# Hash-bucket attention with adapters: output turns by DMA, PSUM copies on VectorE, casts on GpSimd

## The chip, the cores and the metric

The kernel runs on one core of a Trainium2 chip. The metric is the device time of one execution in microseconds (us), lower is better. PE (TensorE), DVE (VectorE), ACT (ScalarE), POOL (GpSimd) and SP (SyncE) each work through their own instructions in order; an instruction that waits holds up all that stand behind it on its engine. SP, ACT and POOL also issue DMAs.

## The reference

There are 4 batches of 8 heads, 768 positions and 64 features a head. Each query and key gets a 6-bit bucket from the signs of its projections; a query attends only to keys of its own bucket. Then comes a mixture of 8 adapters of rank 16, of which each row uses its two best.

```python
q_bits = (np.einsum('bhsd,dk->bhsk', q, proj) > 0)
...
mask = q_bucket[:, :, :, None] == k_bucket[:, :, None, :]
scores = scale * np.matmul(q, k.transpose(0, 1, 3, 2))
scores = np.where(mask, scores, -1000000000.0)
...
attn = attn / (np.sum(attn, axis=-1, keepdims=True) + 1e-09)
x = np.matmul(attn, v)          # heads side by side: 3072 rows x 512
logits = x @ w_gate
topk = np.argpartition(-logits, K, axis=1)[:, :K]
...
delta[mask] += w[mask, k, None] * (z @ B[e])   # z = x[mask] @ A[e]
return (x + delta).astype(np.float32)
```

## The kernel before, in words

The 32 heads go through as 16 pairs (p = 0 to 15), four pairs to a batch. The program is written out by hand: `run` walks over pairs and, in each, over nine slots (s = 0 to 8), and the order in which the calls stand is the order on each engine.

In a slot, `score` (L281) makes 1024 columns of scores on PE, in a PSUM tile of which there are two, and ACT takes their exponential into P (L290). Nine slots make the 2 x 6 blocks of 128 keys by 768 queries of a pair. A score matmul has 71 rows: 64 of features, scaled, and 6 of signs with a constant beside them, so that one matmul gives both the product and the bucket match. These operands lie in `aug`, of which there are two.

Before a pair's scores can run, its q and k are loaded (`load`, two pairs or more ahead, on SP's queue; three buffers), turned on PE in three groups of four blocks (`trans` L208, into a PSUM tile of the pool `ps_t`, which has two), copied from PSUM into `qkT` (two groups by ACT at L222, one by DVE at L224), cast with a factor into `aug` (`cast` L245, two instructions on DVE), and hashed (`hash` L231): PE multiplies with the projections, DVE makes signs (L240) and SP issues four small DMAs that carry them into `aug` (L151).

The output of a head is P turned against v: `pvmm` (L299) works in one PSUM tile (pool `ps_v`, one buffer). v lies in `vb` (three buffers) with a column of ones for the row sums, and a seventh slot that holds the sum of v over the six blocks; `vcast` (L194) makes these on POOL. `pvmm` opens each head with a matmul of the constant `eps` with that seventh slot (L304), which gives the uniform term of rows that match nothing. `norm` (L306) takes the reciprocal of the sums and scales the output into `x` on DVE (L321, L323); after the second head POOL casts x to bf16 (`xb`, L330).

The adapters need x turned: `xtrans` (L353) turns six blocks on PE and copies them into `xT` on DVE (L365). One batch later, in pairs 4b+5 and 4b+6, `moe_slot` (L444) takes three row blocks a pair: `lgz` (logits and first factor, PE), `route_a` and `route_b` (top two and weights on DVE, a small exp on ACT), `zmtrans` (turn), `delta` (second factor, added to x by DVE, L435, and stored).

The last pair orders its queries otherwise, so that a third of the rows is done after three slots; `third` does its output, and the last batch's adapters follow in three groups of two blocks.

## Time and profile before

| | before |
|---|---|
| three runs, median (range) | 196.83 us (196.22 to 197.68) |
| profiled execution, its own time | 195.71 us |
| its span | 193.8 us |
| PE busy | 173.4 us (89%) |
| ACT busy | 159.2 us (82%) |
| DVE busy | 116.6 us (60%) |
| POOL busy | 66.1 us (34%) |
| DMA, mean | 136 GB/s |
| first score, first score of pairs 1, 2 and 15 | 13.0, 23.4, 33.2, 168.4 us |

Busy times come from one profiled execution; matmuls are pipelined and their ends are modelled, so PE's busy share overstates how much of it is used. Durations and starts are read from the groups of instructions, the timeline and the chain of waits. A group's line gives the source line, engine, operation, output and inputs, shapes and count, then the busy time in us and the mean in ns of one, and then the idle time of the engine just before them with what ended it. A line of the chain gives its start, its length and what ran.

### The profile page before, as it was taken

Reading aid. Unit: us, or ns where it says so; the run is one execution under the profiler, and the core shown is the slowest. Engines: PE = TensorE matmul, PEld = TensorE weight load, DVE = VectorE, ACT = ScalarE, POOL = GpSimd, SP = SyncE. Lnnn points to the kernel's source line nnn. Section 1 sums busy time; section 2 is a strip of 40 time slices with the busy share of each in tenths; the row PEclk is TensorE's granted clock in tenths of the full one; section 3 lists DMA queues with packets and bytes.
Section 4 is the critical chain, followed back from the end, with each engine's and each line's share of the span. In section 5 each row is a group of like instructions: output and inputs, shape, how many; then the busy total and the mean of one; then the engine's idle time right before and its main releaser. Section 6 shows DMA issues by size and latency. Waiting matters only on the chain.

```text
span 193.8 us, 5264 instructions
## 1 busy us (share of the span) xinstructions
PE 173.4 (89%) x2176; PEld 118.4 (61%) x2177; DVE 116.6 (60%) x267; ACT 159.2 (82%) x192; POOL 66.1 (34%) x104
## 2 busy tenths in 40 slices
PE   6898899999999999899999999999999999885741
PEld 5464667575766758465758667575758575664520
DVE  4537253637272787866363877783636968824682
ACT  3249899999999897989999998989999988877320
POOL 8189925151506060433333070606060340110000
PEclk9999999999999999999999999999999999999996
DMA  6809960707070706638251608366525221040224
GB/s 162 318 14 194 133 229 11 244 11 244 13 244 14 244 7 172 243 84 332 66 190 39 215 7 261 154 180 235 179 75 175 79 110 63 8 166 0 78 88 162
DMA packets 20953, 26.36 MB, mean 136 GB/s; under 512 B 6210, under 2 KB 19394, under 8 KB 20930
## 3 DMA queue, kind: packets, MB, share of 16 engines
q1 hardware_dynamic: 15950, 25.75, 40.0%
q0 software_dynamic: 4832, 0.27, 4.6%
q8 instruction: 17, 0.28, 0.6%
q14 instruction: 6, 0.05, 0.1%
q10 hardware_dynamic: 148, 0.01, 0.1%
HBM read 19.42 MB, written 6.29 MB: 133 GB/s over the span
## 4 chain that ended last, share of the span: by engine, by line
PE 39%; DVE 17%; ACT 13%; DMA 12%; issue 7%; POOL 6%; SPq 4%; POOLq 0%; DVEq 0%; ACTq 0%
PE s L288 15%; PE pv L295 10%; ACT P L290 9%; DMA nat<-in_k_dram 7%; PE tr L217 5%; DVE aug L249 4%; DMA vn<-in_v_dram 3%; ACT qkT L222 3%; PE xtp L363 3%; PE dl L433 2%; DVE x L323 2%; DVE qkT L224 2%; POOL wa L159 2%; PE pv L304 2%; DVE zm L404 2%
## 5 line engine op out<-in xcount | busy, mean ns | idle before, releaser
L290 ACT ACTIVATE P<-s 128x1024 bf16<-128x1024 f32 x144 | 141.4, 1037 | 14.1 <-PE s L288 13.4
L288 PE MATMUL s<-aug 71*128 71x256 bf16 (+1 forms) x396 | 85.9, 321 | 3.3 <-ACT P L290 2.2
L295 PEld LDWEIGHTS <-P 128*128 128x128 bf16 x1152 | 47.5, 98 | 11.0
L288 PEld LDWEIGHTS <-aug 71*128 71x128 bf16 x396 | 33.9, 98 | 25.2 <-issue 15.1
L295 PE MATMUL pv<-vb,P 128*128 128x65 bf16 x1080 | 47.5, 193 | 0.0
L330 POOL CAST xb<-x 128x768 bf16<-128x768 f32 x15 | 12.4, 825 | 99.4 <-DVE x L323 95.8
L249 DVE TENSOR_SCALAR aug<-qkT 64x1536 bf16<-64x1536 f32 x30 | 28.9, 965 | 10.0 <-ACT qkT L222 9.6
L217 PE MATMUL tr<-ident,nat 128*128 128x128 f32 x180 | 28.7, 278 | 1.2 <-DMA nat<-in_k_dram 1.2
L365 DVE COPY xT<-xtp 128x768 bf16<-128x768 bf16 (+1 forms) x17 | 8.9, 525 | 23.6 <-PE xtp L363 23.6
L217 PEld LDWEIGHTS tr<-ident,nat 128*128 128x128 f32 x180 | 19.9, 140 | 2.6 <-DMA nat<-in_k_dram 2.1
L435 DVE SCALAR_TENSOR_TENSOR acc<-dl,rt,x 128x512 f32<-128x512 f32 x24 | 17.8, 746 | 4.5 <-PE dl L433 3.8
L224 DVE COPY qkT<-tr 128x512 f32<-128x512 f32 x16 | 11.1, 691 | 12.1 <-PE tr L217 12.1
L323 DVE TENSOR_TENSOR x<-pv,ri 128x384 f32<-128x384 f32 x30 | 16.7, 557 | 1.2
L222 ACT COPY qkT<-tr 128x512 f32<-128x512 f32 x29 | 17.2, 595 | 0.0
L201 POOL TENSOR_TENSOR vs<-vn 128x384 f32<-128x384 f32 x16 | 16.0, 998 | 0.0
L199 POOL CAST vb<-vn 128x768 bf16<-128x768 f32 x16 | 13.3, 833 | 4.4 <-DMA vn<-in_v_dram 4.2
L240 DVE TENSOR_SCALAR sgn<-hs 128x384 bf16<-128x384 f32 x15 | 8.3, 552 | 7.7 <-PE hs L237 7.7
L237 PE MATMUL hs<-qkT,proj 128*32 128x384 f32 x120 | 12.8, 498 | 0.0
L304 PE MATMUL pv<-vb,eps 128*128 128x390 bf16 x30 | 10.0, 335 | 1.7 <-DVE x L323 1.7
L433 PE MATMUL dl<-Bcat,zmT 128*128 128x512 bf16 x23 | 8.6, 381 | 1.4 <-ACT zmT L423 0.5
L363 PE MATMUL xtp<-ident_bf,xb 128*128 128x128 bf16 x96 | 8.3, 219 | 1.5 <-DVE xb L351 0.8
L375 PE MATMUL lz<-wa,xT 128*128 128x136 bf16 x96 | 7.5, 223 | 0.3 <-DVE xT L365 0.2
(57 smaller groups left out, 111.3 us busy)
## 6 DMA issues: line engine op xcount, KB each, us to landing
vn<-in_v_dram SPq DMA_DIRECT2D x16, 384.0 KB
nat<-in_q_dram SPq DMA_DIRECT2D x15, 384.0 KB
nat<-in_k_dram SPq DMA_DIRECT2D x15, 384.0 KB
out_dram<-acc SPq DMA_DIRECT2D x6, 768.0 KB
out_dram<-acc SPq DMA_DIRECT2D x6, 256.0 KB
aug<-sgn SPq DMA_DIRECT2D x60, 9.0 KB
nat<-in_q_dram SPq DMA_DIRECT2D x2, 192.0 KB
nat<-in_k_dram SPq DMA_DIRECT2D x2, 192.0 KB
```

The costliest lines, as they stand in the source:

```text
L201: nc.gpsimd.tensor_add(out=s3, in0=vn[:, :, 0:3, :], in1=vn[:, :, 3:6, :])
L217: nc.tensor.transpose(out=ps[:, j * P:(j + 1) * P], in_=self.nat[p][:, idx % 2, idx // 2, u * P:(u + 1) * P], identity=self.ident)
L222: nc.scalar.copy(out=out, in_=ps)
L224: nc.vector.tensor_copy(out=out, in_=ps)
L249: self.nc.vector.tensor_scalar(out=self.aug[p % 2][0:64, :, e * n:(e + 1) * n], in0=self.qkT[p][64 * e:64 * e + 64, :].rearrange("p (j c) ...
L288: nc.tensor.matmul(out=ps[:, o:o + n], lhsT=aug[0:71, 2 * h + 1, kt * P:(kt + 1) * P], rhs=q, start=True, stop=True)
L290: nc.scalar.activation(out=self.P_[p][:, s * 1024:(s + 1) * 1024], in_=ps, func=ACT.Exp, scale=128.0)
L295: self.nc.tensor.matmul(out=pv, lhsT=self.p_at(p, h, kt, i), rhs=self.vb[p % 3][:, h, self.slot(kt), :], start=False, stop=(last and kt == ...
L304: self.nc.tensor.matmul(out=self.pv[p, h], lhsT=self.eps, start=True, stop=False, rhs=self.vb[p % 3][:, h, self.T, :].unsqueeze(1).to_broa ...
L323: nc.vector.tensor_tensor(out=self.x[b][:, :, c:c + D].rearrange("p (u e) d -> p e u d", e=2), in0=pv[:, :, 0:D].rearrange("p (e u) d -> p ...
L363: nc.tensor.transpose(out=ps[:, i * P:(i + 1) * P], in_=self.xb[b][:, sl, hp * P:(hp + 1) * P], identity=self.ident_bf)
L435: nc.vector.scalar_tensor_tensor(out=acc[:, i, :], in0=ps, scalar=self.rt[b, slots][:, i:i + 1], in1=self.x[b][:, slots[i], :], op0=ALU.mu ...
```

## The change

- All three groups of `trans` are copied by DVE, with the factor 2^-5 in the copy; `cast` becomes a plain copy with a change of type on POOL, both halves in slot 1.
- The uniform term leaves `pvmm`. `uniform` computes it once a pair in a small PSUM tile and copies it to SBUF on DVE; `norm` adds it to the PSUM output first.
- `xb` is laid out by pairs, and for pairs 0 to 13 `xturn`, a transposing DMA on SP's queue, takes the place of `xtrans`. It stands in slot 6, ahead of the pair's loads. Pairs 14 and 15 keep `xtrans`.
- `hash` moves from slot 4 to slot 2, the second norm from slot 3 to 4, the loads from slot 5 to 6.
- The adapters of the first two batches are spread over four pairs (2, 2, 1 and 1 blocks); the third batch keeps 3 and 3.
- At the start, the first head's signs go through POOL's and ACT's queues, and scores begin before the second head is hashed; the adapters' weights are loaded in slot 4 of pair 0 and not in slot 1.
- In the last pair `third` is cut in two parts, and the middle third has its PSUM tile in `ps_t`.

```diff
-        self.load_v(1)
 
...
-        turn(0)
+        self.turn0(0)
         for e in range(2):
-            nc.vector.tensor_copy(out=self.proj2[64 * e:64 * e + 64, e:12:2], in_=pst[64 * e:64 * e + 64, :])
-        half(0, 0, True)
+            nc.vector.tensor_copy(out=self.proj2[64 * e:64 * e + 64, e:12:2],
+                                  in_=self.pst[64 * e:64 * e + 64, :])
+        self.half0(0, 0, nc.scalar.copy)
         self.warm(5)
-        hashed(0)
-        half(0, 1, False)
-        turn(1)
-        self.warm(4)
-        hashed(1)
-        half(1, 0, True)
-        half(1, 1, False)
+        self.hash0(0, (nc.gpsimd, nc.scalar))
+        self.half0(0, 1, nc.vector.tensor_copy)
+        self.turn0(1)
+        self.half0(1, 0, nc.gpsimd.tensor_copy)
+        self.half0(1, 1, nc.gpsimd.tensor_copy)
...
-        self.warm(8)
+        self.warm(12)
+
+
+    def turn0(self, h):
+        nc, P = self.nc, self.P
+        for i in range(2):
+            ps = self.ps_s.tile([P, 384], F32, tag="s", name=f"trf{h}_{i}")
+            for u in range(3):
+                nc.tensor.transpose(out=ps[:, u * P:(u + 1) * P],
+                                    in_=self.nat[0][:, i, h, u * P:(u + 1) * P], identity=self.ident)
+            out = self.qkT[0][:, (2 * h + i) * 384:(2 * h + i + 1) * 384]
+            if i:
+                nc.scalar.mul(out, ps, 2.0 ** -5)
+            else:
+                nc.vector.tensor_scalar(out=out, in0=ps, scalar1=2.0 ** -5, scalar2=None, op0=ALU.mult)
+
+    def hash0(self, h, engs):
+        nc = self.nc
+        hs = self.ps_t.tile([self.P, 384], F32, tag="t", name=f"hsf{h}")
+        rows = slice(64 * h, 64 * h + 64)
+        for i in (2 * h, 2 * h + 1):
+            nc.tensor.matmul(out=hs[32 * i:32 * i + 32, :], lhsT=self.proj2,
+                             rhs=self.qkT[0][:, i * 384:(i + 1) * 384], start=True, stop=True)
+        sgn = self.sgp.tile([self.P, 384], BF16, tag="sgn", name=f"sgnf{h}")
+        nc.vector.tensor_scalar(out=sgn[rows], in0=hs[rows], scalar1=0.0, scalar2=0.5,
+                                op0=ALU.is_gt, op1=ALU.subtract)
+        for i in range(2):
+            self.sign_dma(engs[i], 0, 2 * h + i, sgn)
+
+    def half0(self, h, e, copy):
+        copy(out=self.aug[0][0:64, 2 * h:2 * h + 2, e * 384:(e + 1) * 384],
+             in_=self.qkT[0][64 * e:64 * e + 64, h * self.S:(h + 1) * self.S].rearrange("p (j c) -> p j c", j=2))
...
         out = self.qkT[p][:, g * 512:(g + 1) * 512]
         if on_act:
-            nc.scalar.copy(out=out, in_=ps)
+            nc.scalar.mul(out, ps, 2.0 ** -5)
         else:
-            nc.vector.tensor_copy(out=out, in_=ps)
+            nc.vector.tensor_scalar(out=out, in0=ps, scalar1=2.0 ** -5, scalar2=None, op0=ALU.mult)
...
-        self.nc.vector.tensor_scalar(
+        self.nc.gpsimd.tensor_copy(
             out=self.aug[p % 2][0:64, :, e * n:(e + 1) * n],
-            in0=self.qkT[p][64 * e:64 * e + 64, :].rearrange("p (j c) -> p j c", j=4),
-            scalar1=2.0 ** -5, scalar2=None, op0=ALU.mult)
+            in_=self.qkT[p][64 * e:64 * e + 64, :].rearrange("p (j c) -> p j c", j=4))
...
-    def pv_mm(self, pv, p, h, i, last):
+    def pv_mm(self, pv, p, h, i, start, last):
         for kt in range(self.T):
             self.nc.tensor.matmul(out=pv, lhsT=self.p_at(p, h, kt, i),
                                   rhs=self.vb[p % 3][:, h, self.slot(kt), :],
-                                  start=False, stop=(last and kt == self.T - 1))
+                                  start=(start and kt == 0), stop=(last and kt == self.T - 1))
 
     def pvmm(self, p, h, i0, i1):
         if p < 0:
             return
         if i0 == 0:
             self.pv[p, h] = self.ps_v.tile([self.P, self.T, self.D + 1], F32, tag="v", name=f"pv{p}_{h}")
-            self.nc.tensor.matmul(
-                out=self.pv[p, h], lhsT=self.eps, start=True, stop=False,
-                rhs=self.vb[p % 3][:, h, self.T, :].unsqueeze(1).to_broadcast([self.P, self.T, self.D + 1]))
         for i in range(i0, i1):
-            self.pv_mm(self.pv[p, h][:, i, :], p, h, i, i == self.T - 1)
+            self.pv_mm(self.pv[p, h][:, i, :], p, h, i, True, True)
+
+
+    def uniform(self, p):
+        n = self.D + 1
+        ps = self.ps_t.tile([self.P, 2, n], F32, tag="t", name=f"un{p}")
+        self.nc.tensor.matmul(out=ps, lhsT=self.eps, rhs=self.vb[p % 3][:, :, self.T, :], start=True, stop=True)
+        self.uni[p] = self.smallp.tile([self.P, 2, n], F32, tag="uni", name=f"uni{p}")
+        self.nc.vector.tensor_copy(out=self.uni[p], in_=ps)
 
     def norm(self, p, h):
         if p < 0:
...
-            self.xb[b] = self.xp.tile([P, T, self.Dm], BF16, tag="xb", name=f"xb{b}")
+            self.xb[b] = self.xp.tile([P, self.PPB, T, P], BF16, tag="xb", name=f"xb{b}")
             self.xT[b] = self.xp.tile([P, self.nD, self.S], BF16, tag="xT", name=f"xT{b}")
         pv = self.pv[p, h]
+        nc.vector.tensor_tensor(out=pv[:, 0:T, :], in0=pv[:, 0:T, :],
+                                in1=self.uni[p][:, h:h + 1, :].to_broadcast([P, T, D + 1]), op=ALU.add)
         ri = self.smallp.tile([P, T], F32, tag="ri", name=f"ri{p}_{h}")
-        nc.vector.reciprocal(out=ri, in_=pv[:, :, D])
+        nc.vector.reciprocal(out=ri, in_=pv[:, 0:T, D])
         c = (2 * hp + h) * D
         nc.vector.tensor_tensor(
             out=self.x[b][:, :, c:c + D].rearrange("p (u e) d -> p e u d", e=2),
-            in0=pv[:, :, 0:D].rearrange("p (e u) d -> p e u d", e=2),
+            in0=pv[:, 0:T, 0:D].rearrange("p (e u) d -> p e u d", e=2),
             in1=ri.rearrange("p (e u) -> p e u", e=2).unsqueeze(3).to_broadcast([P, 2, T // 2, D]),
             op=ALU.mult)
         if h == 1:
-            c = 2 * hp * D
-            nc.gpsimd.tensor_copy(out=self.xb[b][:, :, c:c + 2 * D], in_=self.x[b][:, :, c:c + 2 * D])
-
-
...
-    def third(self, u):
+            nc.gpsimd.tensor_copy(out=self.xb[b][:, hp], in_=self.x[b][:, :, hp * P:(hp + 1) * P])
+
+
+
+    def third(self, u, part):
         nc, P, T, D = self.nc, self.P, self.T, self.D
         p, b = self.n_pairs - 1, self.B - 1
-        pv = self.ps_v.tile([P, 2, 2, D + 1], F32, tag="v", name=f"pvl{u}")
-        nc.tensor.matmul(
-            out=pv, lhsT=self.eps, start=True, stop=False,
-            rhs=self.vb[p % 3][:, :, T, :].unsqueeze(2).to_broadcast([P, 2, 2, D + 1]))
+        if part == 0:
+            pool, tag = (self.ps_t, "t") if u == 1 else (self.ps_v, "v")
+            pv = pool.tile([P, 2, 2, D + 1], F32, tag=tag, name=f"pvl{u}")
+            ri = self.smallp.tile([P, 2, 2], F32, tag="ri", name=f"ril{u}")
+            self.pvl[u] = pv, ri
+            nc.tensor.matmul(
+                out=pv, lhsT=self.eps, start=True, stop=False,
+                rhs=self.vb[p % 3][:, :, T, :].unsqueeze(2).to_broadcast([P, 2, 2, D + 1]))
+        pv, ri = self.pvl[u]
         for h in range(2):
+            kts = range(T) if h == 0 else range(2) if part == 0 else range(2, T)
+            if h == 0 and part:
+                continue
             for e in range(2):
-                self.pv_mm(pv[:, h, e, :], p, h, 3 * e + u, h == 1 and e == 1)
-        ri = self.smallp.tile([P, 2, 2], F32, tag="ri", name=f"ril{u}")
-        nc.vector.reciprocal(out=ri, in_=pv[:, :, :, D])
-        self.pvl[u] = pv, ri
-        self.third_x(u, self.xb[b])
+                for kt in kts:
+                    nc.tensor.matmul(out=pv[:, h, e, :], lhsT=self.p_at(p, h, kt, 3 * e + u),
+                                     rhs=self.vb[p % 3][:, h, self.slot(kt), :], start=False,
+                                     stop=(part == 1 and e == 1 and kt == T - 1))
+        if part:
+            nc.vector.reciprocal(out=ri, in_=pv[:, :, :, D])
+            self.third_x(u, self.xb[b][:, self.PPB - 1])
 
     def third_x(self, u, dst):
-        D, c = self.D, 2 * (self.PPB - 1) * self.D
+        D = self.D
         pv, ri = self.pvl[u]
         self.nc.vector.tensor_tensor(
-            out=dst[:, 2 * u:2 * u + 2, c:c + 2 * D].rearrange("p e (h d) -> p h e d", h=2),
+            out=dst[:, 2 * u:2 * u + 2, :].rearrange("p e (h d) -> p h e d", h=2),
             in0=pv[:, :, :, 0:D], in1=ri.unsqueeze(3).to_broadcast([self.P, 2, 2, D]), op=ALU.mult)
+
+    def xturn(self, p):
+        if p < 0:
+            return
+        b, hp = p // self.PPB, p % self.PPB
+        self.nc.sync.dma_start_transpose(
+            out=self.xT[b][:, hp, :].rearrange("p (t c) -> p t c", t=self.T),
+            in_=self.xb[b][:, hp].rearrange("p t c -> p (t c)"))
 
     def xtrans(self, p, slots=tuple(range(6)), on_act=False):
         if p < 0:
...
             nc.tensor.transpose(out=ps[:, i * P:(i + 1) * P],
-                                in_=self.xb[b][:, sl, hp * P:(hp + 1) * P], identity=self.ident_bf)
+                                in_=self.xb[b][:, hp, sl, :], identity=self.ident_bf)
         (nc.scalar.copy if on_act else nc.vector.tensor_copy)(
...
-        if s == 0:
+        if b < 0 or b > self.B - 2:
+            return
+        groups = ((0, 1), (2, 3), (4,), (5,)) if b < self.B - 2 else ((0, 1, 2), (3, 4, 5))
+        if g >= len(groups):
+            return
+        slots = groups[g]
+        if s == 1:
             self.lgz(b, slots)
-        if s == 1:
             self.route_a(b, slots)
+        if s == 2:
             self.route_b(b, slots)
         if s == 3:
             self.zmtrans(b, slots)
-        if s in (5, 6, 7):
+        if 0 <= s - 5 < len(slots):
             self.delta(b, slots, s - 5)
 
...
+                if p == 0:
+                    self.first_pair(s)
+                else:
+                    self.pair(p, s)
                 self.moe_slot(p, s)
-        p, b = N - 1, self.B - 1
+        self.last_pair(N - 1, self.B - 1)
+
+    def first_pair(self, s):
+        if s == 0:
+            self.hash0(1, (self.nc.sync, self.nc.sync))
+            self.load_v(1)
+        if s < 3:
+            self.trans(1, s)
+        if s == 3:
+            self.cast(1, 0)
+            self.cast(1, 1)
+            self.load(2)
+        if s == 4:
+            self.hash(1)
+            self.uniform(0)
+            self.load_moe()
+        if s == 5:
+            self.vcast(1)
+            self.load(3)
+        if s == 6:
+            self.pvmm(0, 0, 0, 2)
+            self.trans(2, 0)
+        if s == 7:
+            self.pvmm(0, 0, 2, 4)
+            self.trans(2, 1)
+        if s == 8:
+            self.pvmm(0, 0, 4, 6)
+
+    def pair(self, p, s):
+        if s == 0:
+            self.norm(p - 1, 0)
+            self.trans(p + 1, 2)
+        if s == 1:
+            self.pvmm(p - 1, 1, 0, 2)
+            self.cast(p + 1, 0)
+            self.cast(p + 1, 1)
+        if s == 2:
+            self.hash(p + 1)
+        if s == 3:
+            self.uniform(p)
+            self.pvmm(p - 1, 1, 2, 5)
+        if s == 4:
+            self.pvmm(p - 1, 1, 5, 6)
+            self.norm(p - 1, 1)
+            self.trans(p + 2, 0)
+        if s == 5:
+            self.vcast(p + 1)
+            self.trans(p + 2, 1)
+        if s == 6:
+            self.pvmm(p, 0, 0, 2)
+            self.xturn(p - 1)
+            self.load(p + 3)
+        if s == 7:
+            self.pvmm(p, 0, 2, 4)
+        if s == 8:
+            self.pvmm(p, 0, 4, 6)
+
...
                 self.norm(p - 1, 1)
             if s == 3:
                 self.xtrans(p - 1)
+                self.third(0, 0)
             if s == 4:
-                self.third(0)
+                self.third(0, 1)
             if s == 5:
                 self.xtrans(p, t[0])
-                self.third_x(0, self.x[b])
+                self.third_x(0, x)
                 self.lgz(b, t[0])
             if s == 6:
                 self.route_a(b, t[0])
+                self.third(1, 0)
                 self.route_b(b, t[0])
             if s == 7:
+                self.third(1, 1)
                 self.zmtrans(b, t[0], last=True)
-                self.third(1)
-                self.delta(b, t[0], 0, last=True)
             if s == 8:
                 self.xtrans(p, t[1])
-                self.delta(b, t[0], 1, last=True)
+                self.delta(b, t[0], 0, last=True)
                 self.lgz(b, t[1])
-                self.third_x(1, self.x[b])
+                self.third_x(1, x)
         self.route_a(b, t[1])
+        self.third(2, 0)
+        self.delta(b, t[0], 1, last=True)
         self.route_b(b, t[1])
-        self.third(2)
         self.zmtrans(b, t[1], last=True)
+        self.third(2, 1)
+        self.delta(b, t[1], 0, last=True)
         self.xtrans(p, t[2], on_act=True)
-        self.delta(b, t[1], 0, last=True)
         self.lgz(b, t[2])
+        self.delta(b, t[1], 1, last=True)
         self.route_a(b, t[2])
-        self.third_x(2, self.x[b])
+        self.third_x(2, x)
         self.route_b(b, t[2])
-        self.delta(b, t[1], 1, last=True)
         self.zmtrans(b, t[2], last=True)
         for i in range(2):
             self.delta(b, t[2], i, last=True)
```

## The prediction, made before the changed kernel ran

> **What bounds the kernel now.** I read the stretches of two plain pairs and one adapter pair first (columns: stretch, length, then busy us and count of PE, PEld, DVE, ACT, POOL, and clock, DMA share, GB/s).
>
> ```profile
> 33.30:43.10 9.80, 9.40 (x126) 6.41 (x124) 5.03 (x9) 9.46 (x12) 3.47 (x5) 1.00 0.38 126
> 43.10:52.90 9.80, 9.56 (x126) 6.42 (x124) 5.03 (x9) 9.47 (x12) 3.47 (x5) 1.00 0.40 127
> 63.20:74.00 10.80, 10.67 (x143) 7.33 (x141) 8.63 (x23) 9.81 (x12) 3.47 (x5) 1.00 0.35 114
> ```
>
> A pair without adapter work takes 9.80 us with ScalarE busy 9.46 of them: ScalarE sets it. With adapter work it takes 10.8, PE busy 10.67: PE sets it. VectorE and GpSimd have room (5.0 and 3.5 of 9.8). Then the groups of instructions:
>
> ```profile
> L290 ACT ACTIVATE P<-s 128x1024 bf16<-128x1024 f32 x144 | 141.4, 1037 | 14.1 <-PE s L288 13.4
> L249 DVE TENSOR_SCALAR aug<-qkT 64x1536 bf16<-64x1536 f32 x30 | 28.9, 965 | 10.0 <-ACT qkT L222 9.6
> L222 ACT COPY qkT<-tr 128x512 f32<-128x512 f32 x29 | 17.2, 595 | 0.0
> L323 DVE TENSOR_TENSOR x<-pv,ri 128x384 f32<-128x384 f32 x30 | 16.7, 557 | 1.2
> L330 POOL CAST xb<-x 128x768 bf16<-128x768 f32 x15 | 12.4, 825 | 99.4 <-DVE x L323 95.8
> ```
>
> In a row without gaps exps start every 0.96 us (three in 2.88 in the timeline), so ScalarE's floor in a pair is 9 x 0.963 + 2 copies x 0.48 = 9.63. Last, the chain of waits in pair 7 (start, length):
>
> ```profile
> 92.67 0.45 PE s L288 x2
> 93.12 0.66 SPq L151
> 93.78 0.05 issue
> 93.83 0.72 SPq L151
> 94.56 0.05 issue
> 94.61 0.43 SPq L182
> 95.04 0.05 issue
> 95.09 4.28 DMA nat<-in_k_dram
> 99.37 0.04 issue
> 99.42 0.33 PE tr L217
> ```
>
> SP, which computes nothing, is on the chain: four sign DMAs at 0.72 us each stand ahead of the loads, and the load of k lands just as PE wants to turn it, 4.3 to 5.0 us after its issue. This queue has little slack already.
>
> **What the Trainium skill says.** "VectorE: DVE Perf Modes", The three transpose paths, prices a 128x128 bf16 turn at 1309 ns on the crossbar. "DMA: Bandwidth & Descriptors", Latency and other measured facts, gives a DMA transpose 261 GB/s where the middle dimension isn't contiguous. No DMA transpose is in the trace of before, so nothing here confirms either. "GPSIMD Engine Reference", Engine selection, says that one-input work on GpSimd runs at about line rate and that GpSimd can't reach PSUM. The trace agrees on the rate: the 128x768 cast took 825 ns, 1.07 ns an element.
>
> **The change part by part.** A pair's time zero is PE's start of its first score. PE distances are start to start.
>
> *ScalarE.* All 29 qkT copies leave it, two a pair (0.48 each beside exps): floor 9.63 -> 8.67.
>
> *PE.* From the chain and timeline a plain pair is 9 x 0.435 scores (3.9), 72 x 0.0305 pv (2.2), 3 x 0.475 turns (1.43), hash 0.88, two eps matmuls x 0.17 (0.34), six output turns 0.33: 9.0. Gone are 84 of 96 output turns and 30 eps matmuls of 390 columns. A 130-column one per pair is new (not in the trace; 0.06 to 0.17, I take 0.1). 9.0 - 0.33 - 0.34 + 0.1 = 8.5. Three adapter slots cost 1.45 (12 lz 0.65, ztp 0.17, dl 3 x 0.21), so two cost 1.0 and one 0.5.
>
> *VectorE.* Gone: 28.9 of casts and 14 xT copies x 0.56 = 7.8. New: 29 qkT copies x 0.69 = 20, 30 adds over 390 PSUM elements at 0.56 to 0.62 (row L323 has 384 elements in 0.557) = 18, 15 small uniform copies about 4, four more adapter groups about 4. 116.6 - 36.7 + 46 = 126, some 7.5 us of a 9.6 us pair: not a bound, but each norm grows from 0.8 to about 1.45 us and PE's next pv group waits for it. Two scores and one turn group, 1.4 us, cover that. In PE-bound pairs about 0.3 stays.
>
> *GpSimd.* Two casts of 64x1536 a pair. Between the 293 ns for 128 elements (ident_bf) and 825 for 768 a further element costs 0.83 ns, so 1.5 us each, at worst 2.0. A pair holds 3.0 + 0.83 + 2.75 (v) = 6.6 us. Queued behind the casts is xb, then v's sums.
>
> *Two-engine pace.* Before, the floor of 9.63 became 9.80, and PE's 10.45 in adapter pairs became 11.1 (six from about 10.6 to 11.5). Now ScalarE 8.67 and PE 8.5 lie level, so I take 9.1 for a plain pair, 9.9 with two slots, 9.4 with one, 10.6 with three (bubbles of 0.4 to 0.5; in them the adapters' small exp, which now follows its logits in the same slot, so that the big exps queue behind it). Pairs 2 to 14 hold 3, 4, 4 and 2 of these: 27.3 + 39.6 + 37.6 + 21.2 = 125.7, against 135.2 now (33.18 to 168.42).
>
> *The turned output in SP's queue.* The signs are issued two slots earlier. Hash at 2.4 to 2.9 plus 0.8, sgn 0.56, four issues 3.13: SP is free at about 7.3. The second norm starts after slot 4 (4.5), x ends at 6.2, and the 0.83 cast puts xb at 7.1. So the turn is issued at 7.3, and behind it in SP's order stand this pair's loads. With I for its issue and D for what it delays the loads in the DMA engines: 7.3 + I + 0.48 (q issue) + 4.7 (k landing, mean of 4.28, 4.84, 4.96) + D = 12.5 + x, x = I + D. PE wants that k 4.4 us into the next pair, so a pair lasts **at least 8.1 + x**. Bounds of x: a plain issue is 0.43 and 197 KB at 261 GB/s are 0.75, of which 0.43 hides behind q's own issue: 0.75. At the other end six turns of 1309 ns one after the other: 7.9. Between: 768 pieces of 256 B at the price of the trace's small packets (row q0, 4832 packets at 4.6% of 16 engines' span, 30 ns each) are 1.4 us, so I 0.45 + D 1.0, and I take **x = 1.5**, a floor of 9.6: 3 x 9.6 + 4 x 9.9 + 4 x 9.6 + 2 x 10.6 = 128.0. **Saved in pairs 2 to 14: 7.2.** The adapters read the turned rows four slots after the turn, about 4 us, in pairs 5, 9 and 13 the tightest, so a landing below 4 us costs nothing there.
>
> *The start.* Two separate PSUM tiles end PE's 0.65 wait for the copy between the first turns, and the first score no longer waits for the second head's hash: it goes at about 10.8, not 13.0 (its q signs now by GpSimd's queue, where a small issue took 0.92 and landed in 2.4; v 1's load, moved behind, is wanted only at 24). It is given back: the adapters' weight loads (0.92 + 4.12 + 0.89 of GpSimd) now come after two casts and ahead of v's cast for pair 1. GpSimd: second head's halves to 11.7, v 0 to 15, casts to 18.1, weight loads to 24.0, v 1 to 26.8. PE's uniform matmul of pair 1 stands in slot 3 and waits for that, some 3.5 us. The next score then goes at 27.0, where before it went at 27.65. Five slots at 0.98 against 5.53 us: pair 2 starts at 31.9 against 33.18. **Saved: 1.2.**
>
> *Last pair and tail* (25.4 us). Two longer norms ahead of PE's turn of pair 14: +1.3. The thirds start a slot earlier and in another buffer: the exps of this pair, 8.7 us of work, took 13.8, and of these gaps I give back 2.0. **Saved: 0.7** (between 3 and -1.5).
>
> Sum: 1.2 + 7.2 + 0.7 = 9.1. The profiled execution took 195.71 us (span 193.8 and 1.9 around it): 186.6. The three runs shown lie 0.5 to 2.0 above it, median 1.1, so **187.5**.
>
> **Rivals.**
> *A (forecast), chance 0.33*: x between 1.1 and 2, 185 to 193.
> *B, loads never late, 0.24*: x below 1.1. The pairs keep 125.7, saved 11.4, and with smaller bubbles (13 x 0.25) some 14: 181 to 185. For it: the byte rate. Against: a norm, a cast and an issue now stand ahead of each load.
> *C, a wash, 0.11*: x near 2 with casts of 2 us, which put xb 1 us later (floor 9.1 + x = 11.1): 194 to 199.
> *D, slower, 0.32*: the turn holds SP or the DMA engines, and k of the pair after next lands late in every pair, seen by PE at the first turn group. Break-even: (135.2 + 1.9) / 13 = 10.55, so it decides **from x = 2.4**. At x = 4 pairs 2 to 14 take 157, which makes 216. At 7.9 they take 208, 267. For it: the page's 1309 ns, the chain above, and small pieces: in 64 B ones, as the adapters' weights come, 3072 at 30 ns over 16 engines are 5.8 us. Against: the byte rate above.
>
> Within 1% is what a measurement of this kernel can't tell from no change. Faster gets A, B and a part of C, 0.60; same 0.08; slower 0.32. The range goes from 179 (B with a better tail) to 215, leaving out about 0.03 below and 0.16 above. Case A alone spans 185 to 193.
>
> **What would show it.** ScalarE's busy time near 143 us with no qkT copy, VectorE near 126, GpSimd near 113, some 100 fewer PE instructions in the pairs. Right: PE's wait for nat in slot 4 below 1 us a pair, and one PE wait of about 3.5 us for vb near 23 us. Wrong: the turn's issue row over 2 us, waits of PE's turn group for nat over 2 us a pair, a wait of lz for xT in pairs 5, 9 and 13, or casts far from 1.5 us.

## Result and profile after

The changed kernel takes 204.2 us (median; 203.22 to 205.68), the kernel before 196.79 us (196.22 to 197.68) on the same chip. The ratio is 1.038, with a 95% interval of 1.029 to 1.046: **slower**. The forecast was 187.5 us and faster. A ratio here and below is taken from those runs of a kernel that lie within 1.5% of its fastest, a median from all its runs.

The profiled execution of the changed kernel took 203.36 us, its span is 201.6 (before: 193.8). With PE's first score of pairs 2 and 15 as the cuts, the 7.8 us come from all three stretches:

| us | before | after | difference | forecast |
|---|---|---|---|---|
| up to pair 2 | 33.18 | 34.54 | +1.4 | -1.2 |
| pairs 2 to 14 | 135.2 | 139.5 | +4.2 | -7.2 |
| last pair and tail | 25.3 | 27.5 | +2.2 | -0.7 |

The stretches of a plain pair, a pair with two adapter blocks and one with one (columns: stretch, length, busy us and count of PE, PEld, DVE, ACT, POOL, then clock, DMA share, GB/s):

```profile
34.54:43.51 8.97, 8.81 (x118) 6.18 (x119) 5.30 (x12) 8.68 (x10) 6.39 (x8) 1.00 0.56 161
61.43:73.25 11.82, 9.96 (x129) 6.91 (x130) 8.72 (x23) 9.10 (x11) 7.36 (x10) 1.00 0.58 140
85.10:95.55 10.45, 9.35 (x122) 6.52 (x124) 7.96 (x21) 8.96 (x11) 5.55 (x6) 1.00 0.51 165
```

Plain pairs fell from 9.80 to 8.97 us, below the forecast. With two adapter blocks a pair takes 11.8 and PE is busy for only 10.0 of it: PE is idle for 1.9 us, ACT for 2.7. Before, the first adapter pair, with three blocks, took 11.04 us from first score to first score (62.62 to 73.66), and PE was busy for 10.91. So within pairs 2 to 14 the loss sits in pairs that have adapter work, of which there are now eight in the first two batches instead of four, and it is waiting, not work. The groups that answer those shown of before, with the new add (L324) and the adapters' weights, which the program calls `gw` (L427 now, L403 before; the line of before comes first):

```profile
L403 DVE TENSOR_TENSOR gw<-m,e 128x24 f32<-128x24 f32 x6 | 1.1, 182 | 1.2 <-ACT e L393 1.2
L289 ACT ACTIVATE P<-s 128x1024 bf16<-128x1024 f32 x144 | 141.9, 1023 | 32.3 <-PE s L287 29.6
L249 POOL CAST aug<-qkT 64x1536 bf16<-64x1536 f32 x30 | 43.8, 1460 | 21.8 <-DVE qkT L224 20.9
L224 DVE TENSOR_SCALAR qkT<-tr 128x512 f32<-128x512 f32 x45 | 29.6, 682 | 5.7 <-PE tr L217 5.5
L324 DVE TENSOR_TENSOR pv<-pv,uni 128x390 f32<-128x390 f32 x30 | 17.2, 573 | 21.3 <-PE pv L294 21.2
L427 DVE TENSOR_TENSOR gw<-m,e 128x16 f32<-128x16 f32 (+2 forms) x13 | 8.2, 633 | 1.1 <-ACT e L417 1.1
```

The casts take what they were forecast to (1460 ns). L427 doesn't: it multiplies 8 to 24 numbers a partition and took 182 ns for 24 before; now its mean is 633 and its longest 1070. ScalarE's wait for scores grew from 13.4 to 29.6 us. PE's longest waits (who waits, for whom, us in all, times, the longest), first one line of before:

```profile
PE ztp L419 <- DVE zm L404: 3.4, 4, 1.4
PE ztp L443 <- DVE zm L428: 10.6, 12, 2.2
PE dl L457 <- DVE acc L459: 4.9, 5, 1.0
PE tr L217 <- DMA nat<-in_k_dram: 2.1, 1, 2.1
PE xtp L387 <- POOL xb L335: 1.2, 1, 1.2
```

The wait for `zm` grew from 3.4 to 10.6 us; 3.0 and 4.2 of these lie in the last pair and tail, so in pairs 2 to 14 it grew from 0.4 to 6.4. The chain of waits through the adapter pair that starts at 61.43 (start, length, what; it reads from the hash to the turn of zm, then from a turn of a later pair's blocks to the adapters' second product):

```profile
64.21 0.83 PE hs L237 x8
65.03 0.02 issue
65.06 0.04 DVE sgn L240
65.09 0.44 issue
65.53 0.85 DVE gw L427
66.39 0.02 issue
66.41 0.43 DVE zm L428
66.84 0.05 issue
66.89 0.28 PE ztp L443 x2
...
68.70 0.45 PE tr L217 x4
69.15 1.27 DVE qkT L224 x2
70.42 0.67 DVE acc L459
71.09 0.04 issue
71.13 0.38 PE dl L457
```

Two pieces of VectorE are on the chain. `gw` (L427) lasts 0.85 us. And `acc` (L459), which must read the first product out of the one adapter buffer in PSUM before PE may make the second, stands behind two `qkT` copies of 1.27 us together, which the change put on VectorE.

The queue of SP in a plain pair, where the prediction feared the turn (start, length, line, operation):

```profile
47.30 3.18 SPq L151 DMA_DIRECT2D aug<-sgn  x4
50.83 2.01 SPq L375 DMA_TRANSPOSE xT<-xb  x1
52.88 0.58 SPq L182 DMA_DIRECT2D nat<-in_q_dram  x1
53.51 0.46 SPq L182 DMA_DIRECT2D nat<-in_k_dram  x1
```

The 14 issues of the turn have a median of 1256 ns, this one is the longest. After pair 0 PE never waited for `nat`: even here, q and k issued at 52.88 and 53.51 are turned from 57.22 to 57.85 (the load of k thus lands within some 4.3 us).

Why `gw` is long shows when VectorE's and GpSimd's timelines are laid side by side. First VectorE (start, length, line, operation), in three pairs:

```profile
64.18 0.16 DVE L414 TENSOR_TENSOR m<-lz,top 128x16 f32<-128x16 f32 x1
65.53 0.84 DVE L427 TENSOR_TENSOR gw<-m,e 128x16 f32<-128x16 f32 x1
88.98 1.07 DVE L427 TENSOR_TENSOR gw<-m,e 128x8 f32<-128x8 f32 x1
110.80 0.17 DVE L427 TENSOR_TENSOR gw<-m,e 128x16 f32<-128x16 f32 x1
```

And GpSimd at the same times:

```profile
63.37 2.98 POOL L249 CAST aug<-qkT 64x1536 bf16<-64x1536 f32 x2 [0.80 <-DVE qkT L224]
87.05 2.98 POOL L249 CAST aug<-qkT 64x1536 bf16<-64x1536 f32 x2 [2.23 <-DVE qkT L224]
107.83 2.98 POOL L249 CAST aug<-qkT 64x1536 bf16<-64x1536 f32 x2 [0.98 <-DVE qkT L224]
```

The casts end at 66.35, 90.03 and 110.81. The first two `gw` end at 66.37 and 90.05, the third starts as the casts end and takes its normal 0.17; with half the elements the second takes longer than the first, since it had longer to wait. Of the ten `gw` of pairs 5 to 14 eight are long (0.61 to 1.07 us); all eight start during the second cast of a pair and end 20 to 36 ns after it. The profiler's spans on GpSimd are rough, so no more should be read from these nanoseconds. `m` (L414), in the midst of the first casts, takes its normal 0.16; it has one input in PSUM, while both inputs of `gw` are in SBUF. The Trainium skill, "GPSIMD Engine Reference", Specifications, says that GpSimd's SBUF interfaces are shared with VectorE, with contention for VectorE instructions that have two SBUF inputs. This trace agrees with that, and adds the size: `gw` is held until the cast that runs beside it has ended.

### The profile page after: what moved, and what is told of

The parts are those of the page before. It is cut to its first block, busy times and chain, and to the rows that moved or that the text cites. A ratio compares the mean times of both kernels' runs of the same rounds, so it can differ in the third digit from the quotient of the medians.

```text
span 201.6 us, 5215 instructions
## 1 busy us (share of the span) xinstructions
PE 168.3 (84%) x2072; PEld 116.0 (58%) x2078; DVE 128.4 (64%) x324; ACT 148.0 (73%) x166; POOL 111.0 (55%) x137
## 4 chain that ended last, share of the span: by engine, by line
PE 52%; DVE 19%; POOL 9%; issue 8%; DMA 7%; ACT 2%; SPq 1%; POOLq 0%; DVEq 0%
PE s L287 21%; PE pv L294 9%; PE tr L217 7%; PE hs L237 5%; DVE gw L427 4%; DMA nat<-in_k_dram 3%; DMA xT<-xb 3%; DVE acc L459 3%; DVE zm L428 3%; PE lz L399 3%; POOL vs L201 3%; DVE qkT L224 2%; POOL vb L199 2%; PE ztp L443 2%; POOL xb L335 2%
## 5 line engine op out<-in xcount | busy, mean ns | idle before, releaser
L289 ACT ACTIVATE P<-s 128x1024 bf16<-128x1024 f32 x144 | 141.9, 1023 | 32.3 <-PE s L287 29.6
L287 PE MATMUL s<-aug 71*128 71x256 bf16 (+1 forms) x396 | 88.0, 326 | 3.9 <-issue 1.0
L249 POOL CAST aug<-qkT 64x1536 bf16<-64x1536 f32 x30 | 43.8, 1460 | 21.8 <-DVE qkT L224 20.9
L294 PEld LDWEIGHTS <-P 128*128 128x128 bf16 x1080 | 43.5, 98 | 16.5 <-DVE x L329 6.4
L224 DVE TENSOR_SCALAR qkT<-tr 128x512 f32<-128x512 f32 x45 | 29.6, 682 | 5.7 <-PE tr L217 5.5
L324 DVE TENSOR_TENSOR pv<-pv,uni 128x390 f32<-128x390 f32 x30 | 17.2, 573 | 21.3 <-PE pv L294 21.2
L217 PEld LDWEIGHTS tr<-ident,nat 128*128 128x128 f32 x180 | 21.2, 142 | 5.6 <-DMA nat<-in_k_dram 2.3
L459 DVE SCALAR_TENSOR_TENSOR acc<-dl,rt,x 128x512 f32<-128x512 f32 x24 | 17.8, 747 | 5.6 <-PE dl L457 4.5
L201 POOL TENSOR_TENSOR vs<-vn 128x384 f32<-128x384 f32 x16 | 15.9, 991 | 0.0
L199 POOL CAST vb<-vn 128x768 bf16<-128x768 f32 x16 | 13.2, 825 | 0.1
L237 PE MATMUL hs<-qkT,proj 128*32 128x384 f32 x120 | 12.8, 498 | 0.0
L443 PE MATMUL ztp<-ident_bf,zm 128*128 128x128 bf16 x24 | 3.6, 225 | 10.7 <-DVE zm L428 10.6
L457 PE MATMUL dl<-Bcat,zmT 128*128 128x512 bf16 x18 | 6.8, 378 | 6.0 <-DVE acc L459 4.9
L427 DVE TENSOR_TENSOR gw<-m,e 128x16 f32<-128x16 f32 (+2 forms) x13 | 8.2, 633 | 1.1 <-ACT e L417 1.1
L443 PEld LDWEIGHTS <-zm 128*128 128x128 bf16 x24 | 1.5, 97 | 12.6 <-DVE zm L428 12.6
```

The lines of the kernel that those rows point to most:

```text
L199: nc.gpsimd.tensor_copy(out=vb[:, :, 0:T, 0:D], in_=vn)
L201: nc.gpsimd.tensor_add(out=s3, in0=vn[:, :, 0:3, :], in1=vn[:, :, 3:6, :])
L217: nc.tensor.transpose(out=ps[:, j * P:(j + 1) * P], in_=self.nat[p][:, idx % 2, idx // 2, u * P:(u + 1) * P], identity=self.ident)
L224: nc.vector.tensor_scalar(out=out, in0=ps, scalar1=2.0 ** -5, scalar2=None, op0=ALU.mult)
L237: nc.tensor.matmul(out=ps[32 * j:32 * j + 32, :], lhsT=self.proj2, rhs=self.qkT[p][:, j * 384:(j + 1) * 384], start=True, stop=True)
L249: self.nc.gpsimd.tensor_copy(out=self.aug[p % 2][0:64, :, e * n:(e + 1) * n], in_=self.qkT[p][64 * e:64 * e + 64, :].rearrange("p (j c) -> ...
```

## The experiments

All are edits of the changed kernel. None leaves out a part of the computation.

| kernel | median (range) us | ratio to before (95%) |
|---|---|---|
| changed | 204.2 (203.2 to 205.7) | 1.038 (1.029 to 1.046) |
| gates from PSUM | 201.5 (200.8 to 202.2) | 1.023 (1.016 to 1.030) |
| combine ahead of second copy | 200.3 (198.4 to 200.9) | 1.015 (1.005 to 1.026) |
| both | 197.6 (194.1 to 200.7) | 0.997 (0.991 to 1.003) |
| turns on PE again | 207.3 (203.9 to 210.1) | none |
| casts on VectorE again | 207.1 (205.0 to 207.1) | 1.054 (1.046 to 1.063) |
| adapters over two pairs | 200.4 (196.7 to 202.8) | 1.010 (1.006 to 1.014) |
| both, over two pairs | 197.3 (194.9 to 200.5) | 1.002 (0.999 to 1.005) |
| pair 2's loads at the very start | 207.3 (205.8 to 208.5) | 1.057 (1.048 to 1.066) |
| both, that start, tail edit | 198.7 (197.7 to 199.2) | 1.013 (1.006 to 1.020) |
| pair 2's loads ahead of v of pair 1 | 201.6 (199.2 to 204.3) | 1.022 (1.015 to 1.029) |
| tail edit | 201.3 (199.3 to 202.8) | 1.022 (1.016 to 1.028) |
| both, pair 2's loads ahead of v, tail | 194.5 (191.5 to 195.5) | 0.982 (0.975 to 0.990) |

The median of the kernel before lay between 196.3 and 196.8 us beside them. The changed kernel was not run again beside its edits, which ran on two chips, and the start and the tail vary from execution to execution (below). Pairs 2 to 14 vary less: in the profiles of the changed kernel and of the three edits of its start or tail alone they take 139.5 to 140.1 us. So that stretch is given too where an edit touches it.

### Gates from PSUM

```diff
-        m = self.smallp.tile([P, n, E], F32, tag="m", name=f"m{nm}")
-        nc.vector.tensor_tensor(out=m, in0=lz[:, :, 0:E], in1=top[:, :, 1:2].to_broadcast([P, n, E]),
-                                op=ALU.is_ge)
...
-        nc.vector.tensor_mul(out=gw, in0=m, in1=e)
+        for i in range(n):
+            nc.vector.scalar_tensor_tensor(out=gw[:, i, :], in0=lz[:, i, 0:E], scalar=top[:, i, 1:2],
+                                           in1=e[:, i, :], op0=ALU.is_ge, op1=ALU.mult)
```

> The gates gw are taken from the logits in PSUM and the exp in SBUF in one instruction per block, so that no gate instruction has two SBUF inputs; the mask m is not made. Theory (shared interface: in pairs with adapters gw is held until GpSimd's two casts end, 0.84 to 1.07 us for 8 to 24 elements): gw falls below 0.25 us each, PE's wait of the zm turn for zm falls from 10.6 us to under 6, pairs 5 to 12 shorten by 0.4 to 0.7 us each, some 4 to 6 us in all. Rival (VectorE's queue is simply too full): gw keeps its length or another wait takes its place, under 1.5 us in all. Rival (crossbar turn): no change.

Measured 201.47 us, 2.7 less than the changed kernel. The group of `gw`, first and last start behind the durations:

```profile
L425 DVE SCALAR_TENSOR_TENSOR gw<-lz,top,e x24: 215/218/225, 66.7 to 192.2; 128x8 f32<-128x8 f32 x24
```

With one input in PSUM none of the 24 lasts over 225 ns, though 14 of them start while such a cast runs. The edit also drops the mask `m`, 0.16 us, which was not on the chain above. PE's wait for `zm` fell from 10.6 to 6.7 us (under 6 was expected); one-block pairs of the first batch fell from 10.4 to 9.5 us, two-block pairs from 11.8 to 11.4, and pairs 2 to 14 from 139.5 to 135.5. That is 4.0 us, at the lower end of what was expected; the median shows less.

### Combine ahead of the second copy

```diff
+                if p and s == 5:
+                    self.moe_slot(p, s)
                 if p == 0:
                     self.first_pair(s)
                 else:
                     self.pair(p, s)
-                self.moe_slot(p, s)
+                if s != 5:
+                    self.moe_slot(p, s)
```

> In slot 5 the first delta of the adapters is issued ahead of the second turn group, so that its VectorE step stands before and not behind the second qkT copy. Theory (second part: PE waits about 1 us for acc, which stands behind two qkT copies on VectorE): PE's wait of dl for acc falls from 4.9 us to under 2, two-block pairs shorten by about 0.7 us, 3 to 5 us in all. Rival (shared interface alone): under 1 us.

The second turn group's copy now stands behind the combine; the first group's still stands ahead of it. Measured 200.29 us, 3.9 less. PE's waits for `acc`:

```profile
PE dl L457 <- DVE acc L459: 1.9, 5, 0.4
```

From 4.9 to 1.9 us. Two-block pairs fell from 11.8 to 11.2, and one-block pairs, which have no second product, stayed at 10.4; pairs 2 to 14 fell from 139.5 to 136.6. That is what the chain says: the wait is for the single PSUM buffer between two products.

### Both

> Both edits. If the two waits are independent, the gains add, 7 to 10 us, and the pairs with adapters come to 10 us (two blocks) and 9.6 (one block), total near 195. If one takes the other's place, no more than the larger of the two.

Measured 197.6 us, 6.6 less: the sum of the two (2.7 and 3.9). By the ratios it is 4.1% of the kernel before, against 1.5 and 2.3. Pairs 2 to 14 take 133.3 us instead of 139.5, 6.2 less, against 4.0 and 2.9. The two causes are separate and, but for a little, add; with both edits the kernel is as fast as the one before. The gain expected was 7 to 10. Two-block pairs now take 10.7 to 11.1 (10 expected), one-block pairs 9.5 to 10.1. A part of rival D shows here: the turn's issue takes up to 2.5 us, and PE waits for k in pairs 3, 8 and 12, 0.8 us in all.

### Turns on PE again

```diff
-            self.xturn(p - 1)
             self.load(p + 3)
         if s == 7:
             self.pvmm(p, 0, 2, 4)
+            self.xtrans(p - 1)
```

> The crossbar turn alone is undone: six PE turns and a VectorE copy a pair, in slot 7 as in the kernel before. Theory (the turn is not the cause): plain pairs go from 8.97 to 9.3 us, the total rises by 2 to 5 us. Rival (the turn holds SP's queue or the DMA engines and is the cause): the total falls by 3 us or more.

Measured 207.29 us, but the four runs spread too much for an interval, and the lowest, 203.9, is within the changed kernel's own range. So the times show no gain of the turn, nor the fall by 3 us that the rival asks for. Pairs 2 to 14, at full clock in both profiles, take 142.7 us instead of 139.5: plain pairs 9.13 instead of 8.96, two-block pairs 12.17 instead of 11.8, and PE's wait for `acc` is the same 4.9. The turn on the DMA engines is not what made the kernel slower; in these pairs of the one profile it is worth some 3 us.

### Casts on VectorE again

```diff
-        self.nc.gpsimd.tensor_copy(
+        self.nc.vector.tensor_copy(
             out=self.aug[p % 2][0:64, :, e * n:(e + 1) * n],
```

> The two casts into aug go back from GpSimd to VectorE, nothing else. Theory (shared interface): with no cast on GpSimd in slots 1 to 3 the gates fall to about 0.2 us although VectorE has more to do (two casts of 0.97 us a pair): PE's wait for zm falls, but the casts now stand ahead of the signs and gates in VectorE's queue; total within 2 us of the changed kernel. Rival (VectorE's queue is too full): gw keeps its length and the total rises by over 4 us.

Measured 207.08 us: the time missed, the mechanism held. The first line is the group of `gw`; the second is a wait of PE:

```profile
L427 DVE TENSOR_TENSOR gw<-m,e x13: 156/165/176, 65.8 to 196.5; 128x16 f32<-128x16 f32 x7, 128x8 f32<-128x8 f32 x4, 128x24 f32<-128x24 f32 x2
...
PE lz L399 <- DMA xT<-xb: 3.9, 3, 2.6
```

The same instruction on the same shapes takes 165 ns once GpSimd doesn't make these casts, at most 176. But VectorE's busy time goes from 128 to 149 us, and adapters wait for turned rows; pair 13 alone takes 15.9 us. So of the two places GpSimd is the faster one here, even with `gw` held.

### All adapters over two pairs

```diff
-        groups = ((0, 1), (2, 3), (4,), (5,)) if b < self.B - 2 else ((0, 1, 2), (3, 4, 5))
+        groups = ((0, 1, 2), (3, 4, 5))
```

> The adapters of the first two batches go back to two pairs of three blocks. Theory (the stalls are a price per pair with adapters, not per block: 2.9 us over a plain pair for two blocks, 1.45 for one, 2.5 to 3.0 for three): four pairs cost 5.5 over plain ones and not 8.7, some 6 us less in all. Rival (the work per block costs): no gain, or a loss.

Measured 200.42 us, 3.8 less where some 6 were expected; pairs 2 to 14 take 135.9, 3.5 less. The three-block pairs of the first two batches take 12.1 to 12.5 us, and the two that follow are plain again (9.0 to 9.2): a batch pays twice where the changed kernel pays four times.

### Both edits, over two pairs

> The changed kernel with the gates from PSUM, the combine ahead of the two copies, and all adapters over two pairs of three blocks. Three blocks over two pairs alone gave 200.4 against 204.2 (3.8 saved), the other two edits 197.6 (6.6 saved). If the split over four pairs costs a fixed price a pair that those two edits do not touch: 197.6 - 3.8 = 193.8. If what the split costs is those same two waits, once for each group: 197 to 198.5, since with both edits four pairs of an adapter took 40.3 us together, and two of three blocks (11.4) with two plain ones (8.97) would take 40.7.

Measured 197.34 us, against 197.6 with the split over four pairs; pairs 2 to 14 take 133.1 against 133.3. With the two waits gone the split costs nothing that these runs can tell. It was not wrong in itself; it doubled the number of places where `gw` meets the casts.

### Pair 2's loads at the very start

In the changed kernel SP issues the loads of pair 2 behind the signs of the second head and v of pair 1. The chain of waits at the start:

```profile
14.24 0.19 SPq L151
14.43 0.05 issue
14.48 0.43 SPq L190
14.91 0.06 issue
14.97 0.45 SPq L182
15.42 0.04 issue
15.47 6.28 DMA nat<-in_k_dram
21.74 0.04 issue
21.79 0.33 PE tr L217
```

PE, which got to its first score at 10.55 us instead of 13.0, stands still for pair 2's q and k (0.9 and 2.1 us).

```diff
         self.load_v(0)
+        self.load_v(1)
+        self.load_qk(2)
...
-            self.load_v(1)
...
-            self.load(2)
+            self.load_v(2)
```

> The load of v of pair 1 and of q and k of pair 2 are issued at the very start, ahead of the second head's signs on SP's queue. Theory (the start was given back since PE's turns of pair 2 in slot 6 of pair 0 wait for a load that SP issues only after those signs, and the clock granted to PE falls after that gap): the wait of tr for nat, 3.0 us, vanishes, pair 2 starts near 31.5 and not at 34.5, 2.5 to 3.5 us in all. Rival (the wait is only exchanged for GpSimd's weight loads ahead of v's cast of pair 1): under 1 us.

Measured 207.27 us: a miss, 3 us slower than the changed kernel. PE's waits show why:

```profile
PE s L289 <- DMA aug<-sgnf: 3.5, 1, 3.5
PE un L312 <- POOL vb L206: 1.8, 1, 1.8
```

The wait for k is gone, but the first head's signs, 9 KB each, land later, though they go by other queues than the loads that were moved ahead of them: those on GpSimd's queue, issued at 8.2 in both kernels, land at 13.2 and not at 10.3. The first score goes at 13.4.

### Both edits, that start, and the tail's edit

> Gates from PSUM, first delta ahead of the second turn group, early loads, and for pair 14 the uniform term by a matmul in PSUM again (its norm without the add). If the causes are independent: 197.6 of the first two, less 3 for the start and 1.3 for the two shorter norms at the end, about 193.5, below the kernel before. If they hide each other: 196 or more.

Measured 198.72 us, more than with the two edits alone. The start's edit takes away more than the tail's gives; the wait for the first signs is 5.2 us here.

### Pair 2's loads ahead of v of pair 1 only

```diff
             self.hash0(1, (self.nc.sync, self.nc.sync))
+            self.load_qk(2)
             self.load_v(1)
...
-            self.load(2)
+            self.load_v(2)
```

> The changed kernel with one edit of its start: q and k of pair 2 are loaded right behind the second head's signs, ahead of v of pair 1; v of pair 2 stays where it was. Theory (part of what the start loses is pair 2's k, which landed at 21.79 us because its load stood behind the signs and v of pair 1): k lands 1 to 1.5 us earlier, PE's 3.0 us of waits for q and k of pair 2 fall to about 1.5, first score of pair 2 at 33.3 instead of 34.5, total 203.0 (202.2 to 203.8) against 204.2. Rival (pair 1 is then held by its uniform term, since v of pair 1 lands later): PE's uniform product of pair 1 waits over 1 us and the first score of pair 2 stays at 34.5, total 204.2.

Measured 201.63 us, 2.6 less, which is more than either theory gave. Its profile shows part of each: no wait for q or k of pair 2 is left, but the wait that the rival named stands in its place.

```profile
PE un L310 <- POOL vb L204: 1.7, 1, 1.7
```

In this profiled execution (202.56 us) pair 2 is no earlier than in the changed kernel's (uniform product of pair 2 at 38.10 against 38.06), so how the median gains 2.6 is not settled by it.

### The tail's edit

```diff
+            if p == self.n_pairs - 2:
+                self.nc.tensor.matmul(
+                    out=self.pv[p, h], lhsT=self.eps, start=True, stop=False,
+                    rhs=self.vb[p % 3][:, h, self.T, :].unsqueeze(1).to_broadcast([self.P, self.T, self.D + 1]))
...
-        nc.vector.tensor_tensor(out=pv[:, 0:T, :], in0=pv[:, 0:T, :],
...
+        if p != self.n_pairs - 2:
+            nc.vector.tensor_tensor(out=pv[:, 0:T, :], in0=pv[:, 0:T, :],
...
```

> The changed kernel with one edit of its tail: for pair 14 alone the uniform term is again added on TensorE, as one product into the same PSUM tile for each head, so the two adds on VectorE (573 ns each), the copy of the term and its product go. Theory (the norms of pair 14 with their added step stand on the chain of the last pair: PE waited 1.05 us for x and 1.22 us for xb): the last pair and tail shorten by 1.0 to 1.5, total 202.9 (202.4 to 203.4). Rival (the last pair is held by exponentials and by the slow clock, the norms beside it): total 204.0 to 204.4.

Measured 201.34 us, 2.9 less, more than expected. The stretch that it touches, from the first score of pair 15 on, went from 27.5 to 26.4 us, as expected; but in the profiles without this edit it varies from 26.5 to 29.5. Steadier is the time from the start of the last pair's first exponential to the end of its ninth: 12.8 to 13.0 us in the seven profiles without this edit whose clock doesn't fall meanwhile, 11.7 to 11.9 in the three with it. PE's wait for `xb` is half of what it was, and that for `x` ahead of pair 14's second head fell from 1.05 to 0.44. So the edit saves about 1 us there.

The rest of its profile's gain lies at the start, whose instructions are the same as in the changed kernel: k of pair 2 landed at 19.67 and not at 21.79, and the first score of pair 2 went at 31.14 and not at 34.54. So the start varies by itself, and a gain of 1 to 2 us in the whole can't be read from one profile and these medians.

### Four edits together

The two edits, pair 2's loads ahead of v, and the tail's edit.

> The changed kernel with four edits: gates from PSUM, adapters' combine ahead of the two copies, the tail's edit and this start's edit. If the causes are separate places in time they add: 204.2 - 2.7 - 3.9 - 1.2 - 1.2 = 195.2 (194 to 197), just under the kernel before (196.5). If the start's and the tail's edits give nothing: 197.6 as with the first two alone.

Measured 194.54 us, ratio 0.982 (0.975 to 0.990) to the kernel before: 1.8% less, with an interval that leaves out 1, and within the 194 to 197 that the sum of the gains gave. Against the ratio of the two edits alone, 0.997, the start's and the tail's edit give some 1.5% together; how much each gives is not settled. In its profiled execution (span 193.2) pair 2 starts at 32.6, pairs 2 to 14 take 133.7 us, the last pair and tail 26.9.

## Why the prediction was wrong

The sum was made against profiled times: 186.6 forecast, 203.36 measured, 16.8 us apart. (From 186.6 and the 1.1 above it follows 187.7 and not 187.5, which changes nothing.) By its own steps:

**The pace of pairs with adapters: the step that failed, 13.4 us.** "Bubbles of 0.4 to 0.5" on top of PE's work was carried over from before. A pair with two blocks was to be 9.5 of PE's work and 0.4 of bubbles; its work is 10.0 and its bubbles are 1.9. The stretches give:

| pairs 2 to 14 | forecast (case A) | changed | with both edits |
|---|---|---|---|
| three plain | 28.8 | 26.9 | 27.3 |
| four with two blocks | 39.6 | 47.5 | 43.4 |
| four with one block | 38.4 | 41.6 | 39.2 |
| two with three blocks | 21.2 | 23.5 | 23.4 |
| sum | 128.0 | 139.5 | 133.3 |

Pairs with adapters take 13.4 us more than forecast, the plain ones 1.9 less: 11.5. Of these, 6.2 go with the two edits in the profiles (6.6 by the medians). The prediction priced each adapter instruction at its old duration and looked only at VectorE's and GpSimd's own busy time; it saw neither that `gw` would stand beside GpSimd's casts nor what the new copies on VectorE stand ahead of. The remaining 5.3 us are not taken apart. With both edits PE still waits for `zm` (2.1 us in pairs 2 to 14), 0.8 us for k, and 0.38 us at each of five second products for `acc`, and the changed kernel waited twice for turned rows, 1.0 us in all.

**ScalarE and PE in plain pairs: right.** ScalarE is busy for 8.67 us of a plain pair, as forecast; PE 8.8 (forecast 8.5). The pace is 8.97 where 9.1 was taken. The chain through the three plain pairs now runs over PE alone; ScalarE no longer sets them.

**The turn in SP's queue: right that it is no wait of 2.4 us, wrong as a floor.** x was taken as 1.5 and a pair as at least 9.6. The issue alone is 1.26, near the sum, and 8.1 + 1.26 is already above the 8.97 that a plain pair takes, so other terms of the floor were too long; among them are the 4.7 for k's landing, which took at most some 4.3 in the pair shown. In the changed kernel k of a later pair never came late, so a delay of the loads was not seen: case B's premise held for the loads, and rival D's mechanism, loads held by the turn, did not occur. Only with both edits, where pairs are shorter, k came late three times (0.8 us). The price of 1309 ns a turn that the Trainium skill, "VectorE: DVE Perf Modes", The three transpose paths, states for one block, six times over, would be 7.9 us. The turn of six blocks in pair 8 landed 3.06 us after its issue and another, with both edits, 3.65. So that price can't be multiplied by the blocks here. The prediction's chance of 0.32 for slower rested on that mechanism; slower came by another.

**GpSimd's casts: right in size** (1.46 against 1.5), wrong in that nobody else would feel them.

**VectorE's busy time: right** (128.4 against 126). It is 64% of the span, and still two of its instructions are what PE waits for.

**The start: the sign was wrong.** The first score goes at 10.55, as forecast (10.8). The wait that gives it back was put on GpSimd (3.5 us for v of pair 1); it is the load of pair 2 instead, on SP behind the signs. That wait is 3.0 us, about the size forecast, and after it the clock was at half from 23.3 to 26.7 us (below).

**The tail: the sign was wrong.** The longer norms were counted at +1.3; the tail's edit shows about 1. The exponentials of the last pair took 12.9 us before, not 13.8, a figure that takes in the last one of pair 14. With the short norms of that edit they take 11.7 to 11.9, so about 1 of the 2.0 that the thirds were to give back did come. The term that was put at nothing is what follows the last exponential: 11.7 us before, 13.0 in the changed kernel and 13.0 to 14.2 in the profiles of its edits. Beside that, the clock of the changed kernel's profile was at half from 180.3 to 183.7, and its exponentials took 13.8. Why the end is longer was not tried.

## What to carry to other kernels

When work moves from one engine to another, list for each moved instruction what it shares besides the queue: here a cast on GpSimd held the one VectorE instruction with two SBUF inputs that stood beside it, and a cheap instruction of 16 elements came to stand on the chain that PE waits for. Read one input of such an instruction from PSUM, or stand it where GpSimd is idle. And where an engine gets new copies, ask of each instruction behind them whether it frees a single buffer that another engine wants; moving it ahead of the second of two copies was worth 3.9 us by the medians, 2.9 in pairs 2 to 14, and costs no work.

## What was not expected of the hardware

- A VectorE multiply with two SBUF inputs (128x16 and 128x8, f32) went from 0.17 to as much as 1.07 us and, where it was long, ended within 36 ns of the end of the GpSimd cast beside it. Operations with an input in PSUM beside the same casts did not change (`m` 0.16 us, the adds 0.57).
- The start of the same instruction stream differs by more than 3 us between executions (pair 2 begins at 31.14 to 35.6 us), and the granted clock goes with it. The stretch from 20 to 30 us of the changed kernel, of the one with the tail's edit, and of the one with both edits (clock is the third column from the end):

```profile
20.00:30.00 10.00, 8.21 (x90) 5.61 (x91) 4.25 (x8) 5.71 (x6) 8.11 (x10) 0.83 1.31 164
```

```profile
20.00:30.00 10.00, 9.85 (x135) 6.96 (x134) 6.68 (x13) 8.90 (x10) 9.53 (x12) 1.00 1.27 157
```

```profile
20.00:30.00 10.00, 8.58 (x68) 5.64 (x69) 3.58 (x7) 4.86 (x5) 6.92 (x10) 0.66 1.30 156
```

  The instructions up to there are the same. PE stood still for k for 2.1 us in the first, 0.45 in the second and 2.0 in the third. In the first the clock was at half from 23.3 to 26.7 us, in the third from 21.0 to 27.8. The clock fell where PE had stood still longer; that the one causes the other was not tried.
